# Spectral attention with a feed-forward block on one core: other places for the weights' scan, the filler products, the token norms and the loads

## The chip, the core and the metric

The kernel runs on one core of a Trainium2 chip. The metric is the device time in microseconds of one execution. TensorE (PE) multiplies, VectorE (DVE), ScalarE (ACT) and GpSimd (POOL) work elementwise, SyncE (SP) issues every DMA from one queue that is worked off in order.

## The reference, cut to what matters

```python
# q, k, v: [8, 12, 448, 64] f32; w_ch1: [768, 3072] f64, w_ch2: [3072, 768] f64
scores = q @ k.T / sqrt(64) - log(448)
x = (sigmoid(scores) @ v)             # heads side by side: [8, 448, 768]
u = x + real(fft(fft(x, axis=1), axis=2))
un = (u - mean(u)) / sqrt(var(u) + 1e-6)        # per token, over 768
out = u + relu(un @ w_ch1) @ w_ch2
```

The weights come as 64-bit floats, which the kernel itself turns into 32-bit ones and then into pairs of 16-bit numbers (a high part and the rest), so that each product takes three f16 matmuls (high by high, high by low, low by high).

## The kernel before, in words

There are 3584 tokens in 7 chunks of 512. The program has four stages.

**Attention and mixing (0 to 401 us).** A loop over 168 slots, two per step, makes scores, sigmoids and products with v, and beside them the Fourier mixing of each batch as a list of small units: `psd`, `pss` and the transposes `psx`, each in one of few PSUM banks. A bank is free for the next unit when its reader has run; for `psx` that is the `u` add on DVE (L341). A table `extra` says in which slot every other step stands and with which rank: the loads and casts of q and k (L157 on ACT, L174 `lo` on DVE), the folds, the token norms of chunk 0, and the scan of the 48 weight tiles `wr` of 768 KB. The scan takes of every tile its largest magnitude (`weight_max`, L377) and turns 30 of them into 32-bit floats (`convert`: L385 on ACT, L387 and L390 on DVE), which are stored in `t_dram`. When all 48 are seen, one scale each for w1 and w2 is worked out (`weight_scales`, `scale_product`).

**Plain chunk (401 to about 606 us).** Chunk 0 goes through the feed-forward block, one pair P of 128-wide slices of the hidden layer after the other; P = 2 to 11 here. A pair has 14 ticks; `UPS` puts seven up-products of nine matmuls each (`fast_up`, L992) at ticks 0, 2, 4, 6, 8, 11 and 12. I number them 1 to 7 in that order. They share two PSUM banks: products 1, 3, 5 and 6 accumulate in bank a, products 2, 4 and 7 in bank b. What was in a bank must have been read before the next product goes into it:

- after 1, 3 and 5 ACT copies bank a to `X` (L1007); after 6 ACT takes the relu of it (L1014);
- after 2, 5 and 7 DVE adds `X` and bank b (L1003, `F<-X,psf`). I call these three reads R2, R5 and R7. Product 4 needs R2, product 7 needs R5, product 2 of the next pair needs R7.

Between the up-products stand pieces of the down product of earlier pairs (`down_plain`, L874), as many per tick as `PIECES` says, 12 per pair. In the same ticks DVE, ACT and POOL prepare the weights of the following pairs: w1 words to 32 bits (`w1_turn`: L385, L387, L390), a high part (L560, ACT), a low part (L563, DVE), four sums on POOL (`pair_sum`, L571 `t`), high and low of the rest, and the same for w2 (`w2q`); the results go to `w_dram`. Every engine runs its steps in the order in which the ticks name them (`at_tick`, and `later` for what follows a product; `pin` fixes the order).

**Chunk 1 (606 to about 770 us), P = 12 to 23.** The same with seven products of a fast scheme for the down side too (`fast_down`, L1063; sums in `acc`, L1077). The up weights are loaded again from `w_dram` (`load_w`, L867). For w2 the sums (`w2_sums`: load `cb`, four sums on POOL, L571 `cb`, high L560, low L563, store L863) are made for all 12 pairs here.

**Chunks 2 to 6 (770 to 1617 us).** All weights come from `w_dram`. In every chunk the token norm of the next one is made (`token_norm`, two halves of 128 rows by 2): DVE takes the statistics (L463, L466), the root by small operations of two numbers per partition (L472 to L486), the scaling (L490) and sums and rests (L514, L528); ACT takes the high part (L525).

The tile `wr` of pool `wpre` has three buffers: the first pairs' `tp`, the `cb`, the norm's halves `un16` and the residual rows `ur` (L881) take turns in it.

## Time and profile before

| | us |
|---|---|
| median of 3 runs | 1617.66 (1616.99 to 1619.93) |
| the profiled execution, its own time | 1619.2 |
| its span, first to last instruction | 1617.4 |
| PE busy | 1552.4 (96%) |
| DVE / ACT / POOL busy | 1182.6 / 733.7 / 313.6 |
| mean granted clock of TensorE | 0.984 |

In the rows below a line of the timeline is: start, duration, engine, line and operation, output and inputs, how many were merged, and in brackets how long the engine had been idle and what released it. `PEld` is PE's loading of weights, `SPq` the DMA queue.

### The profile page before, as it was taken

The page shows a single profiled execution, that of the slowest core. Times are in us where ns is not written, and L with a number is a line of the kernel's source. Part 1 is how long each engine was busy: PE and PEld are TensorE (multiplying, and loading weights), DVE is VectorE, ACT ScalarE, POOL GpSimd, SP SyncE. Part 2 cuts the span into 40 slices and gives each one's busy share as a digit, 9 for nine tenths or more (in the row PEclk, how much of TensorE's full clock was granted, in tenths as well). Part 3 has the DMA queues.
Part 4 walks back from the last instruction along what each step waited for, and adds up shares of the span by engine and source line. Part 5 has one row for each costly group of instructions (what it writes and reads, how often), then busy time and mean ns, then how long its engine had stood idle before and what let it go on. Part 6 is the DMA issues. An engine that isn't in the chain of part 4 may idle for free.

```text
span 1617.4 us, 27889 instructions
## 1 busy us (share of the span) xinstructions
PE 1552.4 (96%) x11339; PEld 1076.7 (67%) x11339; DVE 1182.6 (73%) x2035; ACT 733.7 (45%) x1005; POOL 313.6 (19%) x266
## 2 busy tenths in 40 slices
PE   9999999999889897889999999999999999999998
PEld 4555445555566675666777777777777777777775
DVE  2788969646799755787787778776877687766667
ACT  7777767663455434333353335332433252324331
POOL 4656646530223522421000000000000000000000
PEclk9999999999899998999999999999999999999999
DMA  6799898736679788858676867786677667766543
GB/s 229 297 341 332 274 362 291 212 115 240 240 246 332 239 308 320 263 194 268 258 254 236 273 240 236 258 259 236 228 282 233 237 246 264 232 244 230 219 171 147
DMA packets 162995, 407.83 MB, mean 252 GB/s; under 512 B 87489, under 2 KB 101554, under 8 KB 144690
## 3 DMA queue, kind: packets, MB, share of 16 engines
q1 hardware_dynamic: 162866, 406.04, 72.2%
q8 instruction: 89, 1.46, 0.4%
q14 instruction: 40, 0.33, 0.1%
HBM read 319.49 MB, written 66.85 MB: 239 GB/s over the span
## 4 chain that ended last, share of the span: by engine, by line
PE 53%; DVE 4%; POOL 2%; ACT 1%; DMA 1%; issue 1%; POOLq 0%; SPq 0%; ACTq 0%; DVEq 0%
PE pso L1063 26%; PE psf L992 26%; POOL cb L571 2%; DVE F L1003 1%; DVE ws L563 1%; DMA cb<-t_dram 1%; DVE acc L1077 1%; DVE H L1003 1%; ACT H L1032 0%; ACT ws L560 0%; ACT F L1021 0%; DVE acc L1101 0%; DVE un L528 0%; DVE U L514 0%; DVE stt L463 0%
## 5 line engine op out<-in xcount | busy, mean ns | idle before, releaser
L992 PE MATMUL psf<-ut,ws 128*128 128x256 f16 x5166 | 654.5, 275 | 44.5 <-DVE F L1003 22.7
L992 PEld LDWEIGHTS <-ws 128*128 128x128 f16 x5166 | 510.0, 99 | 167.2 <-issue 46.6
L1063 PE MATMUL pso<-ws,H 128*128 128x384 f16 x3024 | 561.2, 327 | 1.0 <-DVE H L1003 0.9
L1063 PEld LDWEIGHTS <-H 128*128 128x128 f16 x3024 | 296.4, 98 | 155.0 <-issue 1.9
L1077 DVE TENSOR_TENSOR acc<-pso,acc 128x384 f32<-128x384 f32 x399 | 220.1, 554 | 87.6 <-PE pso L1063 81.7
L1007 ACT ACTIVATE X<-psf 128x256 f32<-128x256 f32 x246 | 94.0, 382 | 314.5 <-PE psf L992 313.9
L1003 DVE TENSOR_TENSOR F<-X,psf 128x256 f32<-128x256 f32 x246 | 102.7, 417 | 157.5 <-PE psf L992 96.3
L193 ACT ACTIVATE a<-sc 128x900 f32<-128x900 f32 x168 | 148.1, 922 | 57.7 <-PE sc L181 57.5
L1003 DVE TENSOR_TENSOR H<-F,H 128x1024 f16<-128x1024 f32 (+1 forms) x144 | 155.3, 1114 | 6.8 <-ACT H L1032 6.8
L1032 ACT ACTIVATE H<-F 128x1792 f16<-128x1792 f32 x72 | 122.1, 1696 | 67.3 <-DVE F L1003 66.6
L238 PE MATMUL av<-a,vr 128*64 128x450 f32 (+1 forms) x768 | 140.2, 549 | 0.0
L1003 DVE TENSOR_TENSOR F<-F 128x256 f32<-128x256 f32 x288 | 112.2, 428 | 8.8 <-ACT F L1021 6.4
L174 DVE TENSOR_TENSOR lo<-qk,hi 128x834 fp32r<-128x834 f32 (+2 forms) x50 | 59.9, 1202 | 60.4 <-ACT hi L157 57.1
L874 PE MATMUL po<-w2q,H 128*128 128x512 f16 (+1 forms) x528 | 101.4, 336 | 0.0
L238 PEld LDWEIGHTS av<-a,vr 128*64 128x64 f32 (+1 forms) x768 | 44.9, 137 | 83.0 <-issue 78.7
L1014 ACT ACTIVATE F<-psf 128x256 f32<-128x256 f32 x82 | 31.3, 381 | 144.2 <-PE psf L992 144.2
L1021 ACT ACTIVATE F<-F 128x768 f32<-128x768 f32 x72 | 60.6, 842 | 73.2 <-DVE F L1003 73.2
L571 POOL TENSOR_TENSOR t<-t 128x384 f32<-128x384 f32 x40 | 54.7, 1367 | 145.2 <-DVE ws L563 142.9
L571 POOL TENSOR_TENSOR cb<-cb 128x384 f32<-128x384 f32 x48 | 53.9, 1141 | 130.9 <-DMA cb<-t_dram 110.3
L262 POOL TENSOR_TENSOR eo<-xT 128x450 f32<-128x450 f32 x37 | 51.8, 1415 | 101.4 <-ACT xT L250 93.7
L874 PEld LDWEIGHTS <-H 128*128 128x128 f16 x528 | 52.7, 100 | 27.2 <-issue 3.9
L181 PE MATMUL sc<-hi 64*128 64x450 f32 x288 | 62.4, 431 | 0.5 <-ACT a L193 0.5
(122 smaller groups left out, 1524.1 us busy)
## 6 DMA issues: line engine op xcount, KB each, us to landing
ws<-w_dram SPq DMA_DIRECT2D x132, 1344.0 KB, 6.2
wr<-w_in SPq DMA_DIRECT2D x48, 768.0 KB, 8.8
r<-w_in SPq DMA_DIRECT2D x18, 768.0 KB, 7.3
w_dram<-ws SPq DMA_DIRECT2D x10, 1344.0 KB, 8.0
t_dram<-t SPq DMA_DIRECT2D x30, 384.0 KB, 3.1
qk<-q_in SPq DMA_DIRECT2D x48, 225.0 KB, 5.2
qk<-k_in SPq DMA_DIRECT2D x48, 224.0 KB, 7.4
vr<-v_in SPq DMA_DIRECT2D x24, 448.0 KB, 5.5
```

What stands on the lines that cost most here:

```text
L181: nc.tensor.matmul(ps[:, j, :SQ], split[g, kn][1][h, c * 128:(c + 1) * 128], split[g, qn][0][h], start=(n == 0), stop=(n == 2))
L193: nc.scalar.activation(a, ps[:, :, :SQ], AF.Sigmoid, bias=-math.log(S), scale=1.0 / math.sqrt(D))
L238: nc.tensor.matmul(av[1][j * D:(j + 1) * D, :SQ], vr[k, v0:v0 + D], a[k, j], start=(av[0] == 0), stop=(av[0] == 3))
L571: e.tensor_tensor(out=t[:, o], in0=t[:, x], in1=t[:, y], op=op)
L874: nc.tensor.matmul(po[n][:, at:at + hi - lo], h[:, x, j, i * 128:(i + 1) * 128], w[:, y, c0 + lo:c0 + hi], start=(p == j == m == at == 0), ...
L992: nc.tensor.matmul(ps, w[:, i, a, m * 128:(m + 1) * 128], ut[j][:, b + (c == 0), m], start=(no in (1, 2, 5) and m == n == 0), stop=(m == n ...
L1003: nc.vector.tensor_tensor(out=o, in0=x, in1=y, op=op)
L1007: later(0, lambda: nc.scalar.activation(X[:, k], ps, AF.Copy))
L1021: nc.scalar.activation(F[:, 0:3], F[:, 0:3], AF.Relu)
L1032: nc.scalar.activation(h_tile(P)[:, 0], F[:, 1:8], AF.Copy)
L1063: nc.tensor.matmul(ps[:, :384], H[:, x, a, tp * 128:(tp + 1) * 128], w[:, y, b], start=(j == group[0] and n == 0), stop=(j == group[-1] an ...
L1077: later(0, lambda: nc.vector.tensor_tensor(out=to, in0=ps[:, :384], in1=to, op=ALU.add))
```

## The change

The matmuls stay as many as they were. What moves:

- **Scan.** The 48 tiles are spread over slots 22 to 158 instead of 22 to 136, the last eight being the last of w2, and the scale of w1 is worked out at slot 136, that of w2 at 160. Some steps of the scan move by a slot or a rank (`MAX_STEP`, `CONV_STEP`, `CONV_RANK`).
- **Stores** of `u` and of the converted tiles are issued one step of the loop later (`sp_later`).
- **First pairs.** `tp` uses the tile `un` of the mixing pool instead of `wr`.
- **Before the plain chunk** the weights' steps (`prepq`) stand in another order: the load of w2 pair 1 is the fifth step instead of the fourteenth and its use comes after the words of pair 3.
- **Pieces.** Of the 12 down pieces of a pair, 2, 1, 2, 1, 4 and 2 at ticks 1, 3, 5, 7, 10 and 13 become 0, 0, 5, 1, 5 and 1.
- **Ticks.** Tables with fractions give the tick of every preparing step; within a tick a fraction below 0.5 stands before the reads of the products' banks, one above behind them.
- **Norms of chunks 1 to 6** take sums, squares and scaling on ACT (six activations over 768 numbers each per half) and the small operations on POOL, but for three on DVE.
- **Residual rows** of chunk 0 use the pool `first_w2` instead of `wr`.
- **Loads of up weights** are issued three ticks earlier (`LOAD_AT`).

```diff
-PREP = (-6, 10, 14)
+PREP_LEFT = (10, 4)
+PREP = (0, 10, 14)
+SCAN_END = 158
+SCAN_LAST = 8
+SCALES = (136, 160)
...
-PIECES = {1: 2, 3: 1, 5: 2, 7: 1, 10: 4, 13: 2}
+W1P_AT = (1.25, 3, 4, 5.75, 6, 6.25, 9.0, 11.0, 13.0)
+TURN_AT = (2, 4, 4.0, 5.75, 8.0, 8.0)
+W2P_AT = (-4.75, 8.0, 8.0, 9.0)
+SUMS_AT = (-4, 2, 3.0, 6, 8, 10, 10, 11.25, 15.25)
+SUMS2_AT = (-17.0, -10.0, -7.75, -5.0, -3.0, 2.0, 6.25, 9.75, 12.75)
+LOAD_AT = (8.25, 2.0, -2.0)
+NORM0_AT = (6.0, 62.0)
+NORM_AT = (34.0, 90)
+NORM_STEP = (0, 13.0, 17.0, 19.0, 22.0, 22.25, 23.5, 29.25, 29.5, 31.25, 33.25, 34.5, 36.5, 41.5, 43.5)
+PIECES = {1: 0, 3: 0, 5: 5, 7: 1, 10: 5, 13: 1}
...
+            def row_sums(c, n, rows, rest, e):
...
+                if n == 1:
+                    for j in range(2):
+                        nc.scalar.activation(rest, rows[j], AF.Copy, accum_out=mv[:, 5, j:j + 1])
+                    e.tensor_scalar(
+                        out=mv[:, 0], in0=mv[:, 5], scalar1=-1.0 / DM, scalar2=None, op0=ALU.mult)
+                elif n == 2:
+                    for j in range(2):
+                        nc.scalar.activation(
+                            rest, rows[j], AF.Square, bias=mv[:, 0, j:j + 1], accum_out=mv[:, 6, j:j + 1])
...
+                elif n < 7:
+                    rsqrt(c, n - 1, e)
...
+                else:
+                    j = n - 7
+                    nc.scalar.activation(
+                        rows[j], rows[j], AF.Identity, scale=mv[:, 3, j:j + 1], bias=mv[:, 0, j:j + 1])
...
-                when_w.setdefault(22 + n * (TM - 22) // (2 * NFC), []).append(n)
+                when_w.setdefault(22 + n * (SCAN_END - 22) // (2 * NFC), []).append(n)
...
-            for n in (0, 1, 3):
-                at(TP - 10 + (0, 2, 0, 4)[n], lambda n=n: weight_scales(n))
+            for i in range(2):
+                for n in (0, 1, 3):
+                    at(SCALES[i] + (0, 2, 0, 4)[n], lambda n=n, i=i: weight_scales(n, i))
...
             def residual(g):
-                urs[0, g] = u = wpre.tile([128, 2, DM], F32, tag="wr", name="ur", bufs=3)
+                urs[0, g] = u = first_w2.tile([128, 2, DM], F32, tag="q", name="ur", bufs=4)
...
             def later(d, fn):
-                todo.setdefault(now[0] + d, []).append(fn)
+                todo.setdefault(now[0] + d, []).append((0.5, fn))
...
-            prepq += [lambda n=n: w2_pair(0, n) for n in (1, 2, 3)]
-            prepq += [lambda n=n: w1_pair(2, n) for n in range(8)]
-            prepq += [lambda n=n: w2_pair(1, n) for n in (0, 1)] + [lambda: w1_pair(2, 8)]
-            prepq += [lambda: w2_pair(1, 2)] + [lambda j=j, n=n: w1_turn(3, j, n) for j in range(2) for n in range(1, 4)]
-            prepq += [lambda: w2_pair(1, 3)]
+            prepq += [lambda n=n: w2_pair(0, n) for n in (1, 2)] + [lambda: w2_pair(1, 0)]
+            prepq += [lambda n=n: w1_pair(2, n) for n in range(6)] + [lambda: w2_pair(0, 3)]
+            prepq += [lambda n=n: w1_pair(2, n) for n in (6, 7)]
+            prepq += [lambda j=j, n=n: w1_turn(3, j, n) for j in range(2) for n in range(1, 4)]
+            prepq += [lambda: w1_pair(2, 8)] + [lambda n=n: w2_pair(1, n) for n in (1, 2, 3)]
...
             def at_tick(P, k, fn):
-                todo.setdefault(TICKS * (P - 2) + k, []).append(fn)
+                k = TICKS * (P - 2) + k
+                todo.setdefault(math.floor(k), []).append((k % 1, fn))
...
             for P in range(NP, PL + 1):
-                at_tick(P - 1, 1, lambda P=P: load_w(0, P))
+                at_tick(P - 1, LOAD_AT[2], lambda P=P: load_w(0, P))
```

The order on DVE in the attention stage, mixing of batch 2. Before, from the first two to the sixth of its eight reads of `psx` banks (`u<-psx`); `wmax` is the scan, `t` a converted tile, `un` the norm of chunk 0, `eo` and `fd` folds:

```order
L341 TENSOR_TENSOR u<-psx,sm 113x384
L377 TENSOR_REDUCE wmax<-wr 128x1
L514 TENSOR_TENSOR un<-un 128x384 x2
L174 TENSOR_TENSOR lo<-qk,hi 128x834
L341 TENSOR_TENSOR u<-psx,df 112x384
L341 TENSOR_TENSOR u<-psx,sm 112x384
L377 TENSOR_REDUCE wmax<-wr 128x1
L262 TENSOR_TENSOR eo<-xT 128x450
L265 TENSOR_TENSOR fd<-eo 128x450
L387 TENSOR_SCALAR t_1974<-t_1974 128x768
L341 TENSOR_TENSOR u<-psx,sm 113x384
```

Now, in the same place:

```order
L368 TENSOR_TENSOR u<-psx,sm 113x384
L574 TENSOR_TENSOR un<-un 128x384 x2
L199 TENSOR_TENSOR lo<-qk,hi 128x834
L368 TENSOR_TENSOR u<-psx,df 112x384
L368 TENSOR_TENSOR u<-psx,sm 112x384
L289 TENSOR_TENSOR eo<-xT 128x450
L292 TENSOR_TENSOR fd<-eo 128x450
L368 TENSOR_TENSOR u<-psx,sm 113x384
```

Two steps of the scan and one of a conversion no longer stand between these reads; they come later in the program.

The order on DVE in the plain chunk, pair P = 4, the end of what stands between R2 and R5. Before (`mv` is the norm of chunk 1; the last row is R5):

```order
L390 SCALAR_TENSOR_TENSOR t_4545<-r,t_4545 128x768
L472 TENSOR_SCALAR mv<-mv 128x2
L474 TENSOR_SCALAR mv<-mv 128x2
L477 TENSOR_SCALAR mv<-mv 128x2
L387 TENSOR_SCALAR t_4545<-t_4545 128x768
L390 SCALAR_TENSOR_TENSOR t_4545<-r,t_4545 128x768
L482 TENSOR_TENSOR mv<-mv 128x2
L483 TENSOR_TENSOR mv<-mv 128x2
L484 TENSOR_SCALAR mv<-mv 128x2
L486 TENSOR_TENSOR mv<-mv 128x2
L563 SCALAR_TENSOR_TENSOR w2q<-t_4480,wsc,w2q 128x1536
L1003 TENSOR_TENSOR F<-X,psf 128x256
```

Now, the whole of it, from R2 to R5:

```order
L1084 TENSOR_TENSOR F<-X,psf 128x256
L626 SCALAR_TENSOR_TENSOR ws<-t_4394,wsc,ws 128x1152
L418 TENSOR_SCALAR t_4570<-t_4570 128x768
L421 SCALAR_TENSOR_TENSOR t_4570<-r,t_4570 128x768
L418 TENSOR_SCALAR t_4570<-t_4570 128x768
L421 SCALAR_TENSOR_TENSOR t_4570<-r,t_4570 128x768
L626 SCALAR_TENSOR_TENSOR w2q<-t_4477,wsc,w2q 128x1536
L574 TENSOR_TENSOR U<-U 128x384 x2
L1084 TENSOR_TENSOR F<-X,psf 128x256
```

The weights' steps between R2 and R5 are the same six in both. The norm's statistics and small operations are gone from between them; two sums of the norm, which stood in the next pair before, have come in.

The order on SP at P = 12 and 13. Before, from the load of the up weights of P = 13 to that of P = 15:

```order
L867 DMA ws<-w_dram 128x5376
L881 DMA ur<-u_dram 128x2x768 x2
L857 DMA ws<-w_dram 128x2x1152
L863 DMA w_dram<-ws 256x1x1536
L892 DMA y_out<-ur 128x2x768
L857 DMA ws<-w_dram 128x2x1152
L867 DMA ws<-w_dram 128x5376
L863 DMA w_dram<-ws 256x1x1536
L557 DMA cb<-t_dram 128x1536
L892 DMA y_out<-ur 128x2x768
L557 DMA cb<-t_dram 128x1536
L867 DMA ws<-w_dram 128x5376
```

Now, the same three loads of up weights (128x5376):

```order
L938 DMA ws<-w_dram 128x5376
L953 DMA ur<-u_dram 128x2x768 x2
L927 DMA ws<-w_dram 128x2x1152
L938 DMA ws<-w_dram 128x5376
L964 DMA y_out<-ur 128x2x768
L934 DMA w_dram<-ws 256x1x1536
L927 DMA ws<-w_dram 128x2x1152
L619 DMA cb<-t_dram 128x1536 x2
L964 DMA y_out<-ur 128x2x768
L938 DMA ws<-w_dram 128x5376
```

The second load of up weights now stands ahead of the first store of w2 sums and of the first output, the third ahead of the second store.

## Rows read from the trace of the kernel before

**Rows 1.** Busy time in four stages (us, busy and count by engine, granted clock)
```profile
0.00:401.00 401.00, 385.52 (x2597) 215.10 (x2598) 283.64 (x366) 276.37 (x353) 196.28 (x174) 0.98 0.78 269
401.00:606.00 205.00, 183.09 (x1307) 131.24 (x1306) 158.36 (x187) 96.25 (x116) 71.52 (x52) 0.95 0.79 274
606.00:770.00 164.00, 141.60 (x1022) 102.82 (x1021) 120.32 (x209) 64.81 (x88) 45.83 (x40) 0.95 0.77 262
770.00:1560.00 790.00, 790.00 (x6056) 592.31 (x6055) 579.44 (x1197) 284.88 (x432) 0.00 (x0) 1.00 0.70 245
```

**Rows 2.** PE's waits, 0 to 401 us (total, times, longest)
```profile
PE psx L334 <- DVE u L341: 8.8, 6, 3.5
PE psd L301 <- DVE u L341: 1.8, 1, 1.8
...
PE sc L181 <- DVE lo L174: 1.3, 1, 1.3
```

**Rows 3.** PE's waits, 401 to 606 us
```profile
PE psf L992 <- DVE F L1003: 17.3, 8, 3.3
PE psf L992 <- DVE H L598: 4.7, 1, 4.7
```

**Rows 4.** PE's waits, 606 to 770 us
```profile
PE psf L992 <- ACT X L1007: 11.5, 6, 3.6
PE psf L992 <- DVE F L1003: 5.4, 4, 2.6
PE psf L992 <- DMA ws<-w_dram: 5.4, 1, 5.4
```

**Rows 5.** Windows over the twelve stretches at half clock: one, and the sum
```profile
422.39:429.21 6.82, 5.71 (x22) 3.04 (x21) 4.43 (x5) 2.04 (x3) 0.00 (x0) 0.50 0.72 229
...
sum 51.19, PE 47.96 PEld 28.46 DVE 39.23 ACT 18.59 POOL 4.40; mean PE 4.00 PEld 2.37 DVE 3.27 ACT 1.55 POOL 0.37
```

**Rows 6.** Timeline of pair P = 3, from R2 to R5
```profile
432.09 0.42 DVE L1003 TENSOR_TENSOR F<-X,psf 128x256 f32<-128x256 f32 x1 [3.65 <-ACT t L385]
...
433.92 5.87 POOL L571 TENSOR_TENSOR t<-t 128x384 f32<-128x384 f32 x4 [12.42 <-DVE ws L563]
...
437.37 2.77 PE L874 MATMUL po<-w2q,H 128*128 128x512 f16 x18
...
438.86 2.54 DVE L563 SCALAR_TENSOR_TENSOR w2q<-t,wsc,w2q 128x1536 f16<-128x1536 f32 x1
...
441.32 0.41 DVE L1003 TENSOR_TENSOR F<-X,psf 128x256 f32<-128x256 f32 x1
...
441.79 1.14 PE L992 MATMUL psf<-ut,ws 128*128 128x256 f16 x9 [0.66 <-DVE F L1003]
```

**Rows 7.** Timeline at the start of the plain chunk
```profile
405.39 1.57 ACT L560 ACTIVATE w2q<-t,wsc 128x1536 f16<-128x1536 f32 x1 [7.07 <-DMA t<-t_dram]
...
408.23 1.63 PE L992 MATMUL psf<-ut,ws 128*128 128x256 f16 x9 [4.65 <-DVE H L598]
```

**Rows 8.** Timeline of pair P = 16, w2 sums and what follows them
```profile
644.62 12.00 POOL L571 TENSOR_TENSOR cb<-cb 128x384 f32<-128x384 f32 x8 [19.14 <-DVE F L1003]
...
656.65 1.58 ACT L560 ACTIVATE ws<-cb,wsc 128x1536 f16<-128x1536 f32 x1 [4.00 <-POOL cb L571]
...
662.65 1.14 PE L992 MATMUL psf<-ut,ws 128*128 128x256 f16 x9 [2.55 <-ACT X L1007]
```

**Rows 9.** Timeline of the DMA queue: the residual rows' loads
```profile
580.07 15.72 SPq L881 DMA_DIRECT2D ur<-u_dram  x2
```

**Rows 10.** Timeline of DVE: one small operation of the norm, twice
```profile
705.52 0.16 DVE L483 TENSOR_TENSOR mv<-mv 128x2 f32<-128x2 f32 x1
...
712.20 0.92 DVE L483 TENSOR_TENSOR mv<-mv 128x2 f32<-128x2 f32 x1
```

**Rows 11.** Timeline of batch 2's mixing
```profile
184.52 1.34 DVE L387 TENSOR_SCALAR t<-t 128x768 int32<-128x768 int32 x1
...
186.38 0.94 PE L334 MATMUL psx<-ident,xT 128*112 128x128 f32 x4 [1.85 <-DVE u L341]
```

More of the change, by code (lines that the diff above doesn't have):

```diff
@@ L376, in weight_max @@
                 i, f = scan[n]
+                seen_w.add(scan[n])
+                if scan[n] not in ready:
+                    wdone.add(n)
                 nc.vector.tensor_reduce(
@@ L408, in spectral_attention_ffn, with scale_product @@
+            ones = cpool.tile([1, 128], F32, name="ones")
             ws = cpool.tile([128, 4], F32, name="ws")
             big = cpool.tile([128, 2], F32, name="big")
-            wps = []
-            def scale_product(n):
-                wps.append(bank("psw"))
+            wps, seen_w = {}, set()
+            def scale_product(n, i):
+                wps[i, n] = bank("psw")
                 if n == 1:
-                    nc.tensor.transpose(wps[0][:2, :128], wm, ident)
+                    nc.tensor.transpose(wps[i, 1][:1, :128], wm[:, i:i + 1], ident)
@@ L416, in scale_product, with weight_scales @@
                 else:
[L417 to L420 removed]
+                    nc.tensor.matmul(wps[i, 3][:, 0:1], ones, wt2[:, i:i + 1], start=True, stop=True)
+                bank_read(dve_next, lambda: weight_scales(n + 1, i))
+            def weight_scales(n, i):
                 if n == 0:
[L423 removed]
+                    assert all((i, f) in seen_w for f in range(NFC))
+                    nc.vector.tensor_reduce(out=wm[:, i:i + 1], in_=wmax[:, i], op=ALU.max, axis=AX.X)
@@ L453, in weight_scales @@
                     scalar2=2.0 ** -14 / UN_SCALE, op0=ALU.mult, op1=ALU.mult)
-                for i in range(2):
+                for j in range(2):
                     nc.vector.scalar_tensor_tensor(
-                        out=wsc[:, 2:3], in0=big[:, i:i + 1], scalar=3e38, in1=wsc[:, 2:3], op0=ALU.mult, op1=ALU.add)
+                        out=wsc[:, 2:3], in0=big[:, j:j + 1], scalar=3e38, in1=wsc[:, 2:3], op0=ALU.mult, op1=ALU.add)
+            scaled = set()
             mvs = {}
@@ L547, in spectral_attention_ffn @@
             ready = {(i, f) for i in range(2) for f in range(*READY[i])}
-            ripe = sorted(ready)
-            rest_w = [(i, f) for i in range(2) for f in range(NFC) if (i, f) not in ready]
-            scan, nr = [], len(ripe)
-            for n in range(2 * NFC):
-                scan.append((ripe if (n + 1) * nr // (2 * NFC) > n * nr // (2 * NFC) else rest_w).pop(0))
+            final = [(1, f) for f in range(NFC - SCAN_LAST, NFC)]
+            ripe = sorted(ready - set(final))
+            rest_w = [(i, f) for i in range(2) for f in range(NFC) if (i, f) not in ready and (i, f) not in final]
+            scan, nr, ns = [], len(ripe), 2 * NFC - SCAN_LAST
+            for n in range(ns):
+                scan.append((ripe if (n + 1) * nr // ns > n * nr // ns else rest_w).pop(0))
+            scan += final
             prep = {}
```

145 lines of the change are left out of this document (89 added, 56 removed).

## The prediction

> **What bounds the kernel now.** I read the busy time by stage first. From 770 us on PE is busy 790.00 of 790 us at full clock, and the rest of the span to the end is its tail [rows 1]; nothing that DVE, ACT or POOL give up there can shorten it. So all that the change can win lies before 770 us, where PE is idle 15.5, 21.9 and 22.4 us in the three stages [rows 1]. Next I read what PE waited for. In the attention stage it is nearly all DVE: 8.8 + 1.8 us for the `u` adds that free a bank and 1.3 us for a rest, 11.9 us [rows 2]. In the plain chunk it is eight waits for a DVE read of bank b, 17.3 us, and one of 4.7 us [rows 3]. In chunk 1 it is ACT's copies (11.5 us), DVE's reads (5.4 us) and one load (5.4 us), 22.3 us [rows 4]. Together 56.2 us.
>
> Last, the clock. Twelve stretches of the trace, all before 770 us, have the granted clock at 0.50, the lower level of 1.2 GHz; together they last 51.19 us, of which PE was busy 47.96 [rows 5]. Work at half clock takes twice its time, so they cost 47.96 / 2 = 24.0 us. Before the stretch shown PE had stood for DVE's read 3.3 us long (the longest wait of the plain chunk, rows 3). Whoever removes the waits removes these too, in part. The whole pool is 56.2 + 24.0 = 80.2 us.
>
> **The change part by part**, against the profiled execution's own 1619.2 us, which is 1.5 us above the median of 1617.66.
>
> *Attention, scan.* The same 48 maxima and 30 conversions stand in 136 slots instead of 114, 16% fewer per slot, and two of the waits are visibly thinned: in batch 2 a maximum and a shift of 1.34 us, which stood just ahead of the `u` add that PE awaited for 1.85 us [rows 11], come later. What goes there lands after slot 136, at 300 us and beyond, beside the last batches. DVE is busy 283.64 of 401 us [rows 1], so there is room, but it is uneven. I take 5 of the 11.9 us. Bounds: all 11.9 won, or 8 lost, if the late stretch gets waits as dense as those of the middle now. The stores that go out a step later, the tile of the first pairs and the second scale (ten operations on one number per partition) are hidden by the same room; without it they are in the 8.
>
> *Start of the plain chunk.* PE's 4.65 us for `H` came from ACT, which stood 7.07 us for the load of w2 pair 1 ahead of it in its order [rows 7]. That load is now the fifth preparing step instead of the fourteenth, and its use comes after the evacuation. What is late next: the copy after product 1 stands behind one high part of 1.57 us [rows 7], and product 2 now follows product 1 without a filler, so I leave 0.8 us. Gain 3.9.
>
> *Pieces.* This is the largest term. All eight waits of the plain chunk, in the pairs 2 to 9, are product 7 waiting for R5. In pair 3 R2 starts at 432.09, then come a low part, two conversions and the w2 low part of 2.54 us, and R5 starts at 441.32 and ends at 441.73: 9.64 us, against which PE had come 0.66 us too early [rows 6]. Between product 2 and product 7 stood 8 pieces (1, 2, 1, 4), now there are 11 (0, 5, 1, 5). Six pieces are 18 matmuls of full width and narrower ones in equal parts; 18 matmuls took 2.77 us, four pieces' work, so 0.69 us a piece [rows 6]. Three more make R5's slack 2.07 us larger. The mean wait is 17.3 / 8 = 2.16 us and the longest 3.3 [rows 3], so the waits do not all vanish: the longest keeps 1.2 us, and I leave 4.0 us for all eight. The norm's statistics go from between R2 and R5, two sums and a rest come in; I set these against each other. Gain 13.3; all 17.3 if the norm's share is more, and 6 if the margins that paid for it (below) are short.
>
> *The loads in chunk 1.* SP stood 15.72 us in the loads of the residual rows [rows 9], since their buffer of `wr` was taken; behind them waited the up weights of pair 14, for which PE then stood 5.4 us [rows 4]. The residual rows now have a pool of their own and the loads stand ahead of the stores that block the queue. I leave 0.5. Gain 4.9.
>
> *The w2 sums.* In pair 16 POOL did eight sums in 12.00 us, 1.5 each, ACT's high part began right behind them at 656.65, and PE waited 2.55 us for a copy that stood behind it all [rows 8]. Now the even pair's last sum is the sixth instead of the eighth, 3.0 us earlier. Of the 11.5 + 5.4 us [rows 4], 6.0 stay, mostly in pairs 16 and 20, where the norm's small operations go to POOL ahead of the sums and two norm sums stand right before R7. Gain 10.9; bounds 0 (POOL gives back what it saves) and 16.9.
>
> *Norms from 770 us on.* PE has no idle time to give there [rows 1], so nothing is won. ACT gets six activations of 768 numbers per half; 1536 take 1.58 us [rows 8], so 0.8 us each, 4.8 us per half, against ACT's 284.88 us of work in 790 [rows 1]. I cost it at nothing; its cover is the distance between a copy and the product that needs it, and the price without it is a rival below.
>
> *Small operations on POOL.* The same small operation on DVE took 0.16 us alone and 0.92 us while POOL's sums ran [rows 10], so the two engines do hold each other up. The Trainium skill (SBUF — State Buffer, "Who interferes with whom") says that a DVE instruction with two SBUF inputs and a GpSimd one that reads SBUF exclude each other for a whole instruction, the second to issue waiting in full. By that rule moving tiny operations to POOL speaks against the change. If each of the 12 held DVE up as long as the row's difference, 0.76 us, a half would cost 9 us; for the four halves before 770 us that is 36 us, were all of it on R2 to R5. In the new order they stand at the pair's end, not there, and I take nothing.
>
> *Clock.* If about a quarter of the waits stays, I let four of the twelve stretches stay: eight twelfths of 24.0, a gain of 16.0 us. Bounds 4 and 24.
>
> *What I can't see.* A removed wait has often hidden the next: DVE is busy 158.36 of 205 us in the plain chunk [rows 1], and some reads that were early are now due sooner. I put 8 us against that.
>
> Sum: 5 + 3.9 + 13.3 + 4.9 + 10.9 + 16.0 - 8 = 46.0. 1619.2 - 46.0 = 1573.2 for such an execution, 1572 beside the median.
>
> **The rivals.**
>
> *Thin margins (20%).* The three pieces come from the ticks after product 1, 2 and 7. The copy after product 1 had two pieces, product 2 and a piece before product 3, now product 2 alone, 1.14 us (a product's time in rows 6); R7 had four pieces and product 1, now one piece and product 1, 0.69 + 1.14 = 1.83 us. Against it: such a read takes 0.41 us [rows 6]. For it: R7 stands behind a low part that waits for POOL's four sums of 5.87 us [rows 6]. If either is late by 1 us in each of the 11 pairs, and the stretches at half clock of that chunk stay (about 7 us), 18 us are lost: 1572 + 18 = 1590.
>
> *POOL binds (12%).* The sums of chunk 1 stay late since POOL does the norm before them: 10.9 us not won and 5 of the clock's 16: 1572 + 16 = 1588.
>
> *Slower (7%).* ACT works in order. If a norm step on ACT stands unready ahead of a bank's copy, or the copy comes behind 1.6 us of sums each time, PE, which has no idle time from 770 us on, waits. It decides from the point where ACT's extra work between two copies is longer than what lies between a copy and its product, some 3 us. If all 4.8 us of each of the 12 halves reach PE, that is 58 us, more than the 46: 1572 + 58 = 1630. Against it: sums, squares and scaling stand apart, each pair 1.6 us, and behind the copies.
>
> *It does not do what it says (5%).* Waits go from one reader to the next and the time stays within 0.2%, 3.2 us, about what a measurement of this kernel can tell from none.
>
> **How the numbers follow.** The forecast of 1572 has 56%; its own range is 1552 to 1590, and the two rivals that are still faster end near its top or, with some more of the bounds, by 1608. Of the lower bounds, all 80.2 us would give 1537; I don't expect the clock and every wait at once and put the low end at 1546, 26 us below the forecast. The high end, 1608, takes in both rivals with the loss in the attention stage. Outside are the slower case and half of the unchanged one. Faster: 56 + 20 + 12 = 88%, same 5%, slower 7%.
>
> **What would show it.** Right: PE's wait for DVE before product 7 under 6 us in the plain chunk; no wait of more than 1 us for a load of `ws`; the waits for ACT's copies in chunk 1 under 7 us; at most five stretches at half clock; 770 us on unchanged, PE without a gap. Wrong, step by step: waits before products 2 and 3 in every pair 2 to 12 (thin margins); ACT's high part of even pairs still idle for POOL's sums; any PE idle time from chunk 2 on (slower); new `u` waits between 300 and 370 us that outweigh those gone. The forecast fails if PE's idle time before 770 us, now 59.8 us, stays over 35.

## The result and the profile after

The kernel after takes 1572.47 us (median of 4 runs, 1571.36 to 1574.83); the kernel before, run beside it, 1617.33 us (1616.70 to 1619.93). The ratio is 0.9722, with the interval 0.9705 to 0.9738. One of the 40 executions of the kernel before took 1652.56 us at a far lower clock and stands in no comparison. The forecast was 1572 us in a range of 1546 to 1608. The medians differ by 44.9 us; the two profiled executions, from which all that follows is read, have spans of 1617.4 and 1569.6 us and differ by 47.8.

The stages can be compared if both kernels are cut at the same points of their work: where the first up-product of the pairs 2, 12, 14 and 24 begins. First the windows between these cuts in the kernel before (columns as in [rows 1]), then in the kernel after:

```profile
0.00:401.13 401.13, 385.65 (x2597) 215.12 (x2598) 283.64 (x366) 276.37 (x353) 196.28 (x174) 0.98 0.78 269
401.13:580.76 179.63, 157.72 (x1111) 112.17 (x1110) 143.84 (x165) 87.01 (x104) 63.48 (x44) 0.94 0.80 273
580.76:611.92 31.16, 25.77 (x199) 19.28 (x198) 16.46 (x27) 10.08 (x14) 8.04 (x8) 0.97 0.79 302
611.92:770.58 158.66, 141.65 (x1021) 102.91 (x1022) 118.60 (x204) 64.29 (x88) 45.83 (x40) 0.95 0.75 256
770.58:1617.40 846.82, 841.57 (x6415) 627.22 (x6413) 620.04 (x1273) 295.90 (x448) 0.00 (x0) 1.00 0.68 237
```

```profile
0.00:399.12 399.12, 382.98 (x2596) 212.41 (x2597) 286.57 (x377) 276.85 (x355) 201.27 (x174) 0.99 0.79 270
399.12:556.79 157.67, 149.21 (x1111) 108.53 (x1110) 126.81 (x121) 95.47 (x121) 75.43 (x74) 1.00 0.94 312
556.79:582.25 25.46, 25.46 (x200) 19.38 (x199) 14.62 (x22) 9.70 (x13) 7.81 (x8) 1.00 0.90 338
582.25:723.16 140.91, 135.48 (x1023) 100.33 (x1021) 107.89 (x170) 74.60 (x109) 55.40 (x70) 0.99 0.89 289
723.16:1569.60 846.44, 841.55 (x6415) 627.22 (x6413) 583.50 (x1113) 338.79 (x528) 27.90 (x120) 1.00 0.69 238
```

The first number after the window is its length, the next PE's busy time. The 47.8 us came from the pairs 2 to 12 (22.0), 12 to 14 (5.7) and 14 to 24 (17.7); attention gave 2.0, the long stretch from pair 24 on 0.4, though DVE is busy 37 us less there and ACT 43 us more: PE had no idle time to give. Length less busy time is PE's idle time: before 15.5, 21.9, 5.4, 17.0 and 5.3 us, after 16.1, 8.5, 0.0, 5.4 and 4.9. So 30.1 us of idle time went, none of it in attention.

Before the end of the kernel, two stretches are left in which the granted clock is 0.50; before the change there were twelve [rows 5]. Here are the windows over the two and their sum; what counts is PE's busy time, the first number behind the comma, and the clock:

```profile
302.44:309.27 6.83, 4.88 (x16) 2.57 (x18) 3.84 (x6) 6.83 (x10) 5.55 (x4) 0.50 1.05 413
599.40:602.81 3.41, 3.41 (x15) 1.98 (x15) 1.92 (x5) 2.77 (x5) 0.00 (x0) 0.50 0.96 378
sum 10.24, PE 8.29 PEld 4.55 DVE 5.76 ACT 9.59 POOL 5.55; mean PE 4.15 PEld 2.28 DVE 2.88 ACT 4.80 POOL 2.78
```

They cost 8.29 / 2 = 4.1 us in place of 24.0: 19.8 us won. (Work there takes about twice its time: the rows below have an up-product at 2.08 us inside such a stretch, against 1.14 in [rows 6].) PE's busy time without these halves is 1528.4 us before and 1530.5 after, so idle time and clock (30.1 + 19.8) less 2.1 give the 47.8.

What PE still waits for, first in attention (answers to [rows 2]), then from 399 to 557 us ([rows 3]), then from 557 to 723 us ([rows 4]):

```profile
PE psx L361 <- DVE u L368: 4.4, 5, 1.3
PE pss L338 <- ACT A L331: 3.7, 1, 3.7
...
PE psf L1073 <- DVE F L1084: 6.9, 8, 1.6
...
PE psf L1073 <- ACT X L1088: 3.4, 3, 2.3
PE psf L1073 <- DVE F L1084: 1.5, 3, 0.7
PE psf L1073 <- DMA ws<-w_dram: 0.4, 1, 0.4
```

DVE's `F` read holds PE 6.9 us in place of 17.3 (5.9 of them before product 7, in place of all 17.3), the load of `ws` 0.4 in place of 5.4, ACT's copy `X` 3.4 in place of 11.5. In attention the waits for the `u` adds fall to half (4.4 us in place of 8.8), and a new wait of 3.7 us for ACT takes their place.

### The profile page after: what moved, and what is told of

Read it like the earlier page. It is cut to its first block, busy times and chain, and to the rows that moved or that the text cites. A ratio compares the mean times of both kernels' runs of the same rounds, so it can differ in the third digit from the quotient of the medians.

```text
span 1569.6 us, 27940 instructions
## 1 busy us (share of the span) xinstructions
PE 1534.7 (98%) x11338; PEld 1067.9 (68%) x11338; DVE 1119.4 (71%) x1802; ACT 795.4 (51%) x1125; POOL 367.8 (23%) x446
## 4 chain that ended last, share of the span: by engine, by line
PE 78%; DVE 8%; ACT 4%; POOL 4%; issue 3%; DMA 2%; SPq 1%; DVEq 0%; ACTq 0%; POOLq 0%
PE psf L1073 29%; PE pso L1145 28%; PE av L265 7%; PE sc L206 5%; PE psd L328 2%; POOL cb L634 2%; PE po L946 2%; DVE ws L626 1%; PE sc L240 1%; DVE F L1084 1%; ACT ws L623 1%; PE pss L338 1%; PE psx L361 1%; POOL t L634 1%; PE psh L656 1%
## 5 line engine op out<-in xcount | busy, mean ns | idle before, releaser
L1073 PE MATMUL psf<-ut,ws 128*128 128x256 f16 x5166 | 643.1, 273 | 14.1 <-DVE F L1084 8.4
L1084 DVE TENSOR_TENSOR H<-F,H 128x1024 f16<-128x1024 f32 (+1 forms) x144 | 156.3, 1120 | 17.3 <-ACT H L1113 17.2
L265 PE MATMUL av<-a,vr 128*64 128x450 f32 (+1 forms) x768 | 139.9, 547 | 0.0
L529 POOL TENSOR_SCALAR mv<-mv 128x2 f32<-128x2 f32 x12 | 4.2, 346 | 564.5 <-ACT U L528 564.3
L946 PE MATMUL po<-w2q,H 128*128 128x512 f16 (+1 forms) x528 | 93.5, 326 | 0.0
```

Of the source, the lines that this page charges most:

```text
L265: nc.tensor.matmul(av[1][j * D:(j + 1) * D, :SQ], vr[k, v0:v0 + D], a[k, j], start=(av[0] == 0), stop=(av[0] == 3))
L946: nc.tensor.matmul(po[n][:, at:at + hi - lo], h[:, x, j, i * 128:(i + 1) * 128], w[:, y, c0 + lo:c0 + hi], start=(p == j == m == at == 0), ...
L1073: nc.tensor.matmul(ps, w[:, i, a, m * 128:(m + 1) * 128], ut[j][:, b + (c == 0), m], start=(no in (1, 2, 5) and m == n == 0), stop=(m == n ...
L1084: nc.vector.tensor_tensor(out=o, in0=x, in1=y, op=op)
```

## The experiments

Stage lengths of all runs, cut as above, in us; "half" is what the stretches at half clock cost (PE's busy time in them, halved). Both are of one profiled execution. The median stands beside that of the kernel before in the same session. "Clock, all runs" is the span times what the mean granted clock lacks to 1, from the lowest to the highest execution; it also counts PE's idle time in such stretches, and its step is 1.6 us, since the clock is given to three places.

| kernel | median | before | to 2 | 2-12 | 12-14 | 14-24 | from 24 | half | clock, all runs |
|---|---|---|---|---|---|---|---|---|---|
| before | 1617.33 | | 401.1 | 179.6 | 31.2 | 158.7 | 846.8 | 24.0 | 16.1 to 27.6 |
| after | 1572.47 | 1617.33 | 399.1 | 157.7 | 25.5 | 140.9 | 846.4 | 4.1 | 3.1 to 7.9 |
| before, pieces alone | 1610.34 | 1615.40 | 399.6 | 171.4 | 30.4 | 159.1 | 846.8 | 14.0 | 16.1 to 20.9 |
| before, order alone | 1611.35 | 1617.28 | 403.3 | 169.9 | 31.1 | 159.3 | 846.8 | 18.5 | 19.3 to 25.8 |
| before, sums alone | 1606.77 | 1617.28 | 402.0 | 179.7 | 29.3 | 147.2 | 846.8 | 19.3 | 17.6 to 20.9 |
| before, loads alone | 1623.34 | 1618.01 | 399.2 | 175.8 | 30.0 | 163.9 | 846.7 | 13.3 | 16.2 to 27.6 |
| after, old pieces | 1579.81 | 1615.40 | 397.5 | 169.9 | 25.7 | 139.6 | 846.4 | 9.8 | 6.3 to 9.5 |
| after, old sums | 1607.54 | 1615.40 | 401.2 | 156.9 | 31.2 | 172.2 | 846.7 | 17.4 | 19.3 to 20.9 |
| after, norms on DVE | 1589.93 | 1615.40 | 401.7 | 161.9 | 25.5 | 151.5 | 847.2 | 9.6 | 4.8 to 15.9 |
| after, small steps on DVE | 1589.67 | 1618.01 | 401.3 | 160.7 | 25.5 | 153.0 | 848.5 | 7.6 | 6.3 to 9.5 |
| after, scan to 142 | 1582.00 | 1618.01 | 407.9 | 158.7 | 25.5 | 141.8 | 846.7 | 11.4 | 7.9 to 12.6 |
| after, stores at once | 1567.75 | 1618.01 | 395.3 | 158.9 | 25.5 | 139.9 | 846.4 | 0.0 | 0.0 to 1.6 |
| the same, norm steps later | 1569.76 | 1617.28 | 394.9 | 160.2 | 25.5 | 141.0 | 846.4 | 5.0 | 0.0 to 6.3 |
| the same, words earlier | 1572.79 | 1617.28 | 394.7 | 159.9 | 25.5 | 144.6 | 846.5 | 3.3 | 1.6 to 3.1 |

Two things bound what a row of this table can show. The kernel before itself had medians from 1615.40 to 1618.01 us in three sessions, so differences of 2 to 3 us between rows of different sessions are not shown. And four rows (before, and pieces, sums and loads alone) have the same attention code; there the stage goes from 399.2 to 402.0 us and its half clock from 3.4 to 7.8 us. In the five rows with the code of the kernel after (after, old pieces, old sums, norms and small steps on DVE) it goes from 397.5 to 401.7 us. Where a single profile and the clock of all runs differ, the latter is the better witness.

**Pieces alone, and the old pieces in the new kernel.**

```
-PIECES = {1: 2, 3: 1, 5: 2, 7: 1, 10: 4, 13: 2}
+PIECES = {1: 0, 3: 0, 5: 5, 7: 1, 10: 5, 13: 1}
```

> The kernel before with the new row of down pieces (0, 5, 1, 5 in place of 1, 2, 1, 4 ahead of product 7) and nothing else. My theory: the eight waits before product 7 (17.3 us) fall to 4 us or less, no new waits of more than 3 us in sum come before products 2 and 3, and with part of the plain chunk's half clock gone the stage from the first up-product of pair 2 to that of pair 12 falls from 179.6 us to 159 to 165 us; attention stays at 401 us, chunk 1 within 3 us; the total comes to about 1600 us. Rival, thin margins: the three pieces taken from the start and the end of a pair come back as waits before products 2 and 3 of 10 us or more, and the stage keeps over 172 us. Rival, other parts of the change did it (the norm's statistics moved, sums moved): the waits before product 7 stay over 8 us and the stage over 170 us.

Ratio 0.9962 (0.9945 to 0.9979): 5 us, not the 17 that I had expected. PE's waits from pair 2 to 12:

```profile
PE psf L992 <- DVE F L1003: 11.0, 9, 2.0
PE psf L992 <- DVE H L598: 6.1, 1, 6.1
PE psf L992 <- ACT X L1007: 2.4, 5, 1.3
```

Sorted by the product that waited, product 7 has 8.1 us in place of 17.3, but products 2 and 3 of pairs 5 to 11 have 5.4 us that were not there, and the one at the start grew by 1.4. The stage's idle time fell by 2.1 us only. What it did win was clock (from 9.7 us to 2.1 in this stage; over all runs the median fell from 22.6 to 17.7 us, which is the whole gain): its waits are shorter. What my theory said of the waits, the stage and the total was missed, and my 13.3 was too large for this kernel. The thin margins are there, but at half the 10 us that the rival named. The third theory's numbers hold, just (8.1 us against 8, 171.4 against 170): the pieces alone don't do it.

> The kernel after with the old row of down pieces (2, 1, 2, 1, 4, 2) and all else as changed. My theory, pieces are the largest term: waits before product 7 return with 10 us or more in the pairs 2 to 11, half-clock stretches return, and the stage from pair 2 to pair 12 grows from 157.7 us to 168 to 178 us; the total is 12 to 22 us above the kernel after. Rival, the rest of the change (order of the preparation, norm steps, sums) had already made R5 early: the stage stays under 163 us and the total within 6 us of the kernel after.

With all else as changed and the pieces undone, the kernel loses 7 us (1579.81 against 1572.47), and 12.3 us in its own stage of the profile. PE's waits there:

```profile
PE psf L1073 <- DVE F L1084: 13.0, 8, 3.1
```

All 13.0 us are product 7 again. So in the new surroundings the pieces are worth their place: 6.9 us of idle time. The 6.4 us of half clock beside it are of this profile; over all runs the clock cost 6.3 to 9.5 us against 3.1 to 7.9, some 2 us more. The stage is within what I expected, the total is not: this profile and the one of after differ by 3 us the other way outside the stage.

**Order of the preparing steps alone.**

```
-            prepq += [lambda n=n: w2_pair(0, n) for n in (1, 2, 3)]
-            prepq += [lambda n=n: w1_pair(2, n) for n in range(8)]
-            prepq += [lambda n=n: w2_pair(1, n) for n in (0, 1)] + [lambda: w1_pair(2, 8)]
...
+            prepq += [lambda n=n: w2_pair(0, n) for n in (1, 2)] + [lambda: w2_pair(1, 0)]
+            prepq += [lambda n=n: w1_pair(2, n) for n in range(6)] + [lambda: w2_pair(0, 3)]
+            prepq += [lambda n=n: w1_pair(2, n) for n in (6, 7)]
...
```

> The kernel before with the new order of the preparing steps at the start of the plain chunk, and nothing else. My theory: PE's wait of 4.65 us behind the last filler falls to 0.8 us or less, and the stage from pair 2 to pair 12 falls from 179.6 us to 174 to 176.5 us; the waits before product 7 stay at 15 to 18 us. Rival: the load of the w2 pair is as late in the new order because it stands behind the same queue, the wait stays over 3 us. Rival: product 2 now follows product 1 without a filler and waits for its copy, so that the gain is under 2 us.

The 4.65 us of [rows 7] are gone; a wait of 1.9 us before product 6 of the same pair came in their place, and the stage is 9.7 us shorter: 4.9 us of idle time and 4.9 us of clock. The waits before product 7 stay at 15.1 us. The total fell by 5.9 us, so that 4.9 us of idle time and about 1 of clock is the fairer reading: over all runs the clock's median went from 24.2 to 22.5 us only. My 3.9 was the idle time.

**The w2 sums: undone, and alone.**

```
-SUMS_AT = (-4, 2, 3.0, 6, 8, 10, 10, 11.25, 15.25)
-SUMS2_AT = (-17.0, -10.0, -7.75, -5.0, -3.0, 2.0, 6.25, 9.75, 12.75)
+SUMS_AT = (-4, 2, 4, 6, 8, 10, 10, 11, 13)
+SUMS2_AT = (-14, -10, -9, -8, -7, 1, 3, 6, 8)
```

> The kernel after with the old steps of the w2 sums on POOL (the last sum of an even pair is again POOL's eighth of the pair), all else as changed. My theory: ACT's high part of the even pairs 14 to 22 comes about 3 us later, PE's waits for ACT's copies return, and chunk 1 (pair 12 to 24) grows from 166.4 us to 172 to 178 us; the plain chunk moves by under 3 us. Rival, in chunk 1 the pieces and the loads gave it all: chunk 1 stays under 169 us.

It costs 35 us, several times what I expected, and pairs 14 to 24 become longer than in the kernel before. Of the profile's 38.6 us, 26 are idle time and 13 clock. The reason is in the queue. First the DMA queue, POOL and PE in the kernel after, around pair 15, then the same in this one:

```profile
574.43 2.76 SPq L619 DMA_DIRECT2D cb<-t_dram  x2
...
583.44 0.56 SPq L934 DMA_DIRECT2D w_dram<-ws  x1
...
586.08 9.72 POOL L634 TENSOR_TENSOR cb<-cb 128x384 f32<-128x384 f32 x8 [17.89 <-DMA cb<-t_dram]
```

```profile
586.81 0.52 SPq L934 DMA_DIRECT2D w_dram<-ws  x1
587.38 0.61 SPq L619 DMA_DIRECT2D cb<-t_dram  x1
...
589.88 0.67 SPq L619 DMA_DIRECT2D cb<-t_dram  x1
...
601.38 5.99 POOL L634 TENSOR_TENSOR cb<-cb 128x384 f32<-128x384 f32 x6 [3.45 <-DMA cb<-t_dram]
...
612.74 2.08 PE L1073 MATMUL psf<-ut,ws 128*128 128x256 f16 x9 [9.26 <-ACT X L1088]
```

The first number of `SUMS2_AT` is the step of the load of `cb`. At -17 both loads go out together, ahead of the store `w_dram<-ws`, which must wait for its result; at -14 they stand behind it. POOL's second half then begins at 601.38. ACT's high part, which stands ahead of the copies in ACT's order, waits for it for 11.38 us, the copy comes behind, and PE stands for 9.26 us before product 3 of pair 15; so it does in pairs 19, 21 and 23 (4.5, 3.7 and 6.2 us). I had read the term off POOL's order (sixth sum instead of eighth); by these rows the load's place in SP's queue is the larger part. That is read, not shown: no run moves the load alone back to -14.

> The kernel before with the new steps of the w2 sums, rounded to whole ticks (the kernel before knows no fractions), and nothing else. My prediction's term: the even pair's last POOL sum comes 3 us earlier, PE's waits for ACT's copies in chunk 1 fall from 11.5 us to under 6, and pairs 14 to 24 fall from 158.7 us to 148 to 152 us, the total by 7 to 10 us. Rival, suggested by the undoing that cost 35 us (more than the waits of before): the sums' new steps pay only together with the earlier loads and the norm off DVE; alone they move pairs 12 to 24 by under 3 us. Rival, they are worse alone, since the words of the next pair are asked for three ticks earlier and take a buffer from the residual rows: the stretch from pair 12 to 14 grows by 2 us or more.

Alone, with the steps rounded to whole ticks, it is worth 10.5 us (ratio 0.9930, 0.9905 to 0.9955), a little more than the 7 to 10 expected: pairs 14 to 24 fall to 147.2 us (6.9 us of idle time, 3.3 of clock), the copies' waits to 1.3 us. Neither rival holds. The waits for the load of `ws` grow, from 5.4 us in one wait to 7.8 in three.

**The loads alone.**

```
-urs[0, g] = u = wpre.tile([128, 2, DM], F32, tag="wr", name="ur", bufs=3)
+urs[0, g] = u = first_w2.tile([128, 2, DM], F32, tag="q", name="ur", bufs=4)
-                at_tick(P - 1, 1, lambda P=P: load_w(0, P))
+                at_tick(P - 1, -2, lambda P=P: load_w(0, P))
```

> The kernel before with two edits: the residual rows are loaded into the buffers that the w2 pairs had (no wait for the third buffer of wr), and the up weights of the next pair are issued three ticks earlier. My theory: PE's wait of 5.4 us for the up weights of pair 14 falls to 0.5 us or less, the stretch from pair 12 to pair 14 falls from 31.2 us to 26 us, nothing else moves by more than 3 us, and the total falls by about 5 us. Rival, the loads are late for another reason (the stores behind which they queue): the wait stays over 3 us. Rival, ACT's high parts and POOL's sums are next in line: the wait goes, and another of 3 us or more appears in the pairs 13 to 15.

This part alone makes the kernel slower: ratio 1.0031 (1.0019 to 1.0044), so the third theory holds. Its profiled execution (1617.4) is the shortest of its ten, with the least half clock; its idle time is 9 us above that of the kernel before, 8.6 of them in the pairs 14 to 24. First ACT and PE at the start of pair 13, then the queue, POOL and PE around pair 15:

```profile
592.17 0.36 ACT L1014 ACTIVATE F<-psf 128x256 f32<-128x256 f32 x1
592.58 1.14 PE L992 MATMUL psf<-ut,ws 128*128 128x256 f16 x9 [2.74 <-ACT F L1014]
...
602.58 0.52 SPq L863 DMA_DIRECT2D w_dram<-ws  x1
603.15 0.60 SPq L557 DMA_DIRECT2D cb<-t_dram  x1
...
616.87 6.00 POOL L571 TENSOR_TENSOR cb<-cb 128x384 f32<-128x384 f32 x6 [4.10 <-DMA cb<-t_dram]
...
628.23 2.08 PE L992 MATMUL psf<-ut,ws 128*128 128x256 f16 x9 [8.24 <-ACT X L1007]
```

SP's 15.72 us in the residual rows ([rows 9]) are gone, and so is the wait of 5.4 us for `ws`. A wait of 2.7 us before product 1 of pair 13 is new: ACT's relu of bank a stands behind a high part that waits for POOL's sums (with the old sums in the new kernel the same wait is 3.9 us). And the loads of `cb` still stand behind the store, while PE comes earlier: it waits 8.24 us there in place of 3.6. The loads and the sums are one edit in two places.

**The norms back on DVE, whole and the small steps alone.**

```
-                            lambda fn: later(1, fn), nc.gpsimd))
+                            lambda fn: later(1, fn), nc.vector))
```

and for the whole norm also `if c and n < 9` made false, so that DVE takes the statistics and the scaling.

> The kernel after with the norms of chunks 1 to 6 back on DVE (statistics by DVE, the small steps on DVE in place of POOL), at the steps the change gives them. My theory: from the first up-product of pair 24 on nothing moves (846.4 us within 1.5 us), since PE has no idle time there; before it the total moves by under 3 us either way, by way of the waits of 1.59 and 1.50 us before product 7 in the pairs 4 and 8, where ACT's scaling had waited for POOL's small step of 1.0 to 1.3 us: they go if POOL was the cause, and others may come from DVE. Rival, the move of the norms off DVE is what made R5 early: the waits before product 7 come back with over 8 us in the plain chunk and the total grows by 8 us or more.

> The kernel after with only the small operations of the late norms on DVE in place of POOL; the row sums, squares and scaling stay on ACT. It splits the 15 us that came back when the whole norm went back to DVE (plain chunk 157.7 to 161.9 us, pairs 14 to 24 140.9 to 151.5 us). Theory A, DVE's statistics are what was dear: the time stays within 3 us of the kernel after, and PE's waits of 1.59 and 1.50 us before product 7 of the pairs 4 and 8 fall under 1 us, since ACT's scaling no longer waits for POOL's step of 1.0 to 1.3 us. Theory B, POOL's small steps stand in the wrong place whoever runs them, or DVE has no room for them beside R5: those waits stay and the total grows by 5 us or more. Theory C, the rule that DVE and POOL hold each other up is what costs in the kernel after: the total falls by 3 us or more.

Both lose 17 us (1589.93 and 1589.67 against 1572.47). So the move of sums, squares and scaling to ACT brought nothing that can be told from none (0.3 us by the medians, 2 us by the ratios); the small steps, fifteen per half, brought it all. My first theory failed, its rival's numbers hold (8.1 us of waits before product 7 against 8), and of the second run's theories B holds. From pair 24 on the stage grew by 0.7 us with the whole norm on DVE, as expected, and by 2.1 us with the small steps alone. First DVE and PE in pair 20 with the small steps on DVE, then POOL in the kernel after:

```profile
678.88 0.92 DVE L517 TENSOR_TENSOR mv<-mv 128x2 f32<-128x2 f32 x1
679.83 0.93 DVE L518 TENSOR_SCALAR mv<-mv 128x2 f32<-128x2 f32 x1
...
685.02 0.17 DVE L518 TENSOR_SCALAR mv<-mv 128x2 f32<-128x2 f32 x1
...
687.10 2.08 PE L1073 MATMUL psf<-ut,ws 128*128 128x256 f16 x9 [5.33 <-DVE F L1084]
```

```profile
669.69 0.20 POOL L517 TENSOR_TENSOR mv<-mv 128x2 f32<-128x2 f32 x1
...
670.67 10.15 POOL L634 TENSOR_TENSOR cb<-cb 128x384 f32<-128x384 f32 x8
```

On DVE the steps lie beside POOL's sums (674.49 to 683.71 us there) and take 0.92 and 0.93 us; the same step takes 0.17 us once the sums are over. The sixteen from 676 to 686 us take 7.4 us, where 0.17 each would make 2.7. They stand between DVE's `F` reads, and PE waits 5.33 us before product 4, which needs R2. On POOL they come ahead of the sums on the same engine, here 0.19 to 0.37 us each.

How much of the 17 us is this holding up isn't shown. Up to 770 us the steps on DVE take 10.1 us more than 0.17 each; the rest may be their plain place between the reads, and no run has them on DVE while POOL rests. Nor does the move end the meeting: on POOL 11 of the 60 steps take 0.66 to 1.31 us beside DVE's work, but few of them stand before something that PE waits for. They may in pairs 4 and 8; here POOL, ACT and PE in pair 4 of the kernel after:

```profile
433.81 1.30 POOL L516 TENSOR_TENSOR mv<-mv 128x2 f32<-128x2 f32 x1
...
438.08 1.95 ACT L543 ACTIVATE U<-U,mv 128x768 f32<-128x768 f32 x2 [2.62 <-POOL mv L540]
...
445.30 1.14 PE L1073 MATMUL psf<-ut,ws 128*128 128x256 f16 x9 [1.59 <-DVE F L1084]
```

With the small steps on DVE the two waits stay, 1.41 and 1.76 us, so POOL's step is not the whole of their cause.

**The scan to slot 142.**

```
-SCAN_END = 158
+SCAN_END = 142
```

> The kernel after with the weights' scan ending at step 142 in place of 158 (the same 48 maxima and 30 conversions in 120 slots in place of 136); the rest as changed. My theory as corrected by the traces: the longer scan won next to nothing in the waits of the attention stage (its idle time is 15.5 us before and 16.1 us after, and four profiles of the same attention code ranged from 397.5 to 401.7 us), so the stage stays at 397 to 403 us and the total within 3 us of the kernel after. Rival, the prediction's term: the denser scan brings u waits back and the stage grows by 4 us or more.

It loses 9.5 us, 8.8 of them in attention (in this profile 3.1 of idle time, most of the rest clock): the rival, my prediction's own term, was right, and the correction I had made of it wrong. PE's waits in attention:

```profile
PE psx L361 <- DVE u L368: 8.3, 6, 2.7
...
PE psd L328 <- DVE u L368: 2.6, 1, 2.6
```

The `u` waits are back at 8.3 us, near the 8.8 of [rows 2], and the half clock of this stage is 9.7 us in place of 2.4. Over all runs the clock cost 7.9 to 12.6 us in place of 3.1 to 7.9. It isn't the old scan exactly: that ended at slot 136, and the steps of single tiles and the late second scale were kept. So the scan did win, and something else in the change took it back; the next run has part of it.

**The stores at once.**

```
-STORES = (1, 1)
+STORES = (1, 0)
```

> The kernel after with the stores of the converted tiles issued in the next slot, as before, and not one slot later. The kernel after has one long attention wait, 3.70 us before the shift product at 304.4 us: ACT's convert step waited 5.79 us for its buffer, whose store SP issued only at 296.5 us. My theory: with the store one slot (about 2.2 us) earlier that wait falls to under 2 us and the half-clock stretch of 6.8 us behind it goes; attention falls by 3 to 5 us. Rival, SP itself is the cause (it stood 7.2 us in one transposing load at 287.5 us): the store stays behind that, the wait stays within 1 us, and the total within 3 us of the kernel after, or is above it because the transposing loads now stand behind stores.

1567.75 us, ratio 0.9692 (0.9676 to 0.9707), 4.7 us under the kernel after; the highest of its executions (1568.80) lies below the lowest of that kernel (1571.36). First the kernel after, then this one: the transposing load and the store on SP, ACT's convert step, PE.

```profile
287.45 7.23 SPq L591 DMA_TRANSPOSE ut<-un  x2
...
296.52 0.42 SPq L433 DMA_DIRECT2D t_dram<-t  x1
...
302.24 0.89 ACT L416 ACTIVATE t<-wr 128x768 f32<-128x768 f32 x1 [5.79 <-DMA t_dram<-t]
...
304.38 1.63 PE L338 MATMUL pss<-A,cs_sb 113*113 113x385 f32 x2 [3.70 <-ACT A L331]
```

```profile
288.41 6.88 SPq L591 DMA_TRANSPOSE ut<-un  x2
295.38 0.53 SPq L433 DMA_DIRECT2D t_dram<-t  x1
...
300.28 0.90 ACT L416 ACTIVATE t<-wr 128x768 f32<-128x768 f32 x1 [3.46 <-DMA t_dram<-t]
...
302.43 0.90 PE L338 MATMUL pss<-A,cs_sb 113*113 113x385 f32 x2 [1.39 <-ACT A L331]
```

The store stays behind the transposing load, as the rival said, but it now goes out first behind it, 1.1 us earlier; the wait falls by 2.3 us and the half clock behind it doesn't come. No stretch at half clock is left before the end. The idle time of attention falls by 2.0 us; most of the rest is clock.

**Two more steps on top of it.** The scaling and the `U` sums of the norm later, and then the load of `cb` earlier as well:

```
-NORM_STEP = (..., 29.25, 29.5, 31.25, 33.25, ...)
+NORM_STEP = (..., 30.75, 30.75, 31.75, 33.75, ...)
```

```
-SUMS2_AT = (-17.0, ...)
+SUMS2_AT = (-20.0, ...)
```

> The kernel after with the stores at once (which alone brought 1572 down to 1568 us) and the norm's scaling and U sums 0.5 to 1.5 ticks later: the scaling behind ACT's high part of w2 and behind the X copy, the sums behind R5. My theory: the waits before product 7 in the pairs 4 and 8 (1.58 and 1.52 us), where ACT's scaling had waited 2.6 us for POOL ahead of the high part, fall to 0.5 us or less; the plain chunk falls by 2 to 3 us from 158.9 us; the total is 1565 to 1566 us. Rival: what is moved behind R5 stands ahead of R7 or of the next pair's R2 and waits of the same size come before product 4 or 2: the total stays within 1 us of 1568 or rises.

> The same as the run with stores at once and later norm steps, and besides the load of the words for the w2 sums of odd pairs three ticks earlier. In the kernel after POOL stood 17.9 us for such a load before pair 15, ACT's high part waited 4.8 us for POOL, and PE 2.3 us for the copy behind it. My theory: the load is queued behind others on SP, three ticks (about 3.4 us) bring POOL's start forward by 1 to 3 us, PE's wait in pair 15 falls under 1 us, the total falls by 1 to 2 us against the other run. Rival: the load needs a buffer that is not free yet, so SP stands for it and the loads behind it come later: the wait stays or grows and other loads are late, total 0 to 5 us higher.

Neither helps: 1569.76 and 1572.79 us. The waits before product 7 of pairs 4 and 8 are gone, but what was moved behind R5 stands ahead of R7. DVE and PE at the start of pair 5 in the first of the two:

```profile
444.34 1.02 DVE L574 TENSOR_TENSOR U<-U 128x384 f32<-128x384 f32 x2
445.28 0.41 DVE L1084 TENSOR_TENSOR F<-X,psf 128x256 f32<-128x256 f32 x1
...
445.75 1.14 PE L1073 MATMUL psf<-ut,ws 128*128 128x256 f16 x9 [1.71 <-DVE F L1084]
```

The wait of 1.6 us became one of 1.7 us, before product 2. With the load at -20 the copy's wait in pair 15 grew from 1.91 to 2.96 us, and pairs 14 to 24 by 3.6 us. The load itself went out only 0.5 us earlier, at 572.18 in place of 572.71 us and behind the same entries of SP's queue, and POOL's sums began later, by the profile behind DVE's `H`; what made them late is not shown. The best kernel of all runs is the one with the stores at once.

## Why the prediction was right, point by point

The terms without the clock sum to 30.0 us, and the idle time that went is 30.1; the clock was put at 16.0 and gave 19.8. That it fits so closely is in part luck. Attention fell short of its 5 by 5.6 us and the plain chunk of its 17.2 by 3.8, chunk 1 gave 1.2 more than its 15.8 and the rest 0.4: together 7.8 us missing, and the 8 us set against "what I can't see", to which no row gave a size, happened to cover them. The clock's 3.8 us too many are partly offset by 2.1 us of longer busy time and by the profiles differing by more than the medians.

- *Attention, 5 of 11.9: mis-sized.* Idle time there rose from 15.5 to 16.1 us. The term was meant without the clock, and in idle time the scan is worth 3.1 us by its undoing, while the stores, which I had called "hidden by the same room", took 2.0 back. With the clock the two are 9.5 and 4.7 us. Some 2.8 us (9.5 - 4.7, less the 2.0 that the stage did win) are not accounted for; profiles with the same attention code lie up to 4.2 us apart (397.5 to 401.7).
- *Start of the plain chunk, 3.9: right.* Measured alone 4.9 us of idle time; the 4.65 us wait is 0.4 now.
- *Pieces, 13.3: the right step, too large.* Waits before product 7 fell from 17.3 to 5.9 us (under 6, as written), but by the pieces alone only to 8.1, and with new waits at products 2 and 3; undoing them brings back 7.1 us there. The stage's idle time fell by 13.4 us, 4.2 of them at the start, so 9.2 are left for the pieces and what else moved on DVE. The thin margins came in three pairs of the kernel after, 1.8 us at products 2 and 3. The price of a piece stands, though its words are wrong: six pieces are 24 matmuls, and the 18 of [rows 6] are the four pieces named beside them.
- *Loads, 4.9: right in size* (5.4 us of idle time, 5.7 of length), *wrong as a separate term*: alone the edit costs 5 us, since ACT's high parts still wait for late sums.
- *w2 sums, 10.9: right in size* (idle 17.0 to 5.4 us), alone 10.5 us with the clock. The step named was, by the rows, the smaller one: the load's place ahead of the store seems to count more than the sixth sum for the eighth.
- *Norms from 770 us on, nothing: right*, 0.4 us. The slower rival's mechanism, a step that stands unready on ACT ahead of a copy, shows before 770 us: small in pairs 4 and 8, large with the old sums and with the loads alone, where a high part is that step.
- *Small steps on POOL, nothing: wrong.* They are worth 17 us in the new order, and they are fifteen per half, not twelve. I had weighed the rule of the Trainium skill (SBUF — State Buffer, "Who interferes with whom") as one that speaks against the move, with a price of up to 36 us. The rows show DVE's steps with two inputs held up beside POOL's sums, as the rule has it (0.92 us against 0.16 for L517); but the steps met those sums while they were on DVE, and the move takes them out of the way of DVE's reads. On POOL some are held up too, where PE mostly doesn't wait for them. I had the rule's sign wrong for this change.
- *Clock, 16 of 24: right*, 19.8; two stretches are left where I allowed five. The wait of 3.3 us named with the stretch of [rows 5] doesn't end before it: the clock falls inside that wait. Over all runs it cost 16.1 to 27.6 us before and 3.1 to 7.9 after.

The rival "POOL binds" did not come: the sums are early because their load is. The old sums in the new kernel are late by way of that load and not of POOL's norm; they cost 35 us, where I gave the rival 16.

## What to carry to other kernels

Edits of a schedule are not terms of a sum: four of them alone gave 5, 6, 10 and -5 us, 16 together, and the whole, which has the scan, the norms and the finer ticks besides, gave 45; of the whole, pieces, sums, small steps and scan undone one by one cost 7, 35, 17 and 10, 69 together. A step that loads is judged by what stands ahead of it in its queue, above all a store that waits for a result. Where small work is held up beside large work on another engine, ask which of the two engines the bottleneck waits for: here moving the small work off that engine won 17 us, though it was still held up at times.
